# Row values spread by VectorE, and V of four head groups made 512 columns wide in two rounds over its weights

## The chip, the cores and the metric

The kernel runs on one core of one Trainium2 chip. The metric is the device time of one execution in microseconds; several executions are timed and their median counts. One further execution is profiled, and its trace is what the views below are taken from.

## The reference

Two attention layers with 32 heads of 32 columns, on 2048 rows of width 1024 each, and their outputs side by side. Layer A looks at 8 keys, two positions apart; layer B at a sliding block of 256 keys:

```
qkv = (x @ wqkv).reshape(B, S, 3, H, Dh)
# A: keys at s, s-2, ..., s-14
logits = einsum("bhsd,bhswd->bhsw", q, kg) * scale
attn = softmax(where(mask, logits, -1e9));  o = einsum("bhsw,bhswd->bhsd", attn, vg)
# B: 0 <= s - t < 256
scores = einsum("bhqd,bhkd->bhqk", q, k) * scale
p = softmax(where(mask, scores, -1e9));     o = einsum("bhqk,bhkd->bhqd", p, v)
out = concatenate([A: o @ wo, B: o @ wo], axis=-1)
```

All of it is float32.

## The kernel before

**Units and groups.** The work is cut into 8 units of 512 rows: four of layer B ("dense"), then four of layer A, whose even and odd rows are sorted apart, so that its dilated window becomes a plain one of 8 ("window"). Each unit has 8 groups of four heads. For one group the kernel computes q and k (`qk_items`, L333 to L424), stacks them in `qst` and `kst`, makes two passes over the scores (`attention` L656, `window` L546), multiplies by V and hands the result to the output product (`o_items`, L487).

**Precision.** A float32 operand is split on the chip into a high and a low part of TensorE's rounded type (`Stream.parts`, L160: a cast, then two subtractions of 512 columns, on VectorE). A product is three matmuls, `TERMS` (L32): high by high, high by low, low by high. In the scores the parts are stacked instead: rows 0 to 95 of `qst` and `kst` hold high and low parts of 32 columns, three deep, written by DMAs on SP's queue (`place`, L369 to L375).

**Two passes and the row values.** The first pass (`first`, L666) computes a block of scores for 128 rows, VectorE finds each row's masked maximum (L686) and ScalarE the sum of exponentials (L691). `log_sum` (L702) makes one number per row of it, again as high and low part. `rows` (L718) transposes these 16 x 2 columns by a matmul with the identity (L720) into 32 rows of PSUM; VectorE copies them to `rt` (L724), and one DMA on SP's queue (L727) lays them as rows 96 and 97 of `qst`. In `kst` these two rows hold ones (L283). So the second pass (`second`, L559 and L755), which contracts over 98 rows, has the row values already subtracted, transposed, and ScalarE needs only an exponential (L573, L770). Four PSUM banks serve scores of both passes and the transposed row values (ring `rs`); one of them is given back when `rt` is copied.

**V.** `VPARTS` (L25) cuts a unit's V into four parts of two groups, 256 columns each. A part (`v_items`, L436) goes through eight slices of the contraction; in each it computes four blocks of 128 rows, two to a PSUM bank, so that two banks (of three in ring `rg`) are in use. The input block is the stationary operand and the weights, 256 columns, the moving one (L464). Its weights are two items of 128x1024. Each finished bank is copied into `vbuf` (L474).

**Weights.** All weights and inputs are one list of items in the order of use. An item is loaded by a DMA on POOL's queue into one of three raw buffers (L137), split on VectorE (L163, L171) and kept in one of three weight buffers. `split_to` has the next item split while the current one is used.

**The order.** The program is straight-line; its order is worked out when it is built. `plan` (L204 to L215) lists the large products: for each unit and slot s the two output products of the unit before (`O_SLOTS`), q and k of group s, and after that the V part that `V_SLOTS` (L26; for unit 0 `V0_SLOTS`, L28) gives to the slot. The inputs of the next unit are split inside the part of slot 7. Four queues of work stand beside each other: row values, second passes, first passes and large products. A loop (L872) always takes the one whose next piece can start first, by a model of the engines (`Clock`, L35) with a duration for each instruction and a due time for each transfer. Instructions are issued to every engine in the order that this loop gives.

Of the kernel before, what the change touches and what calls it, by code (L numbers as in the profile page):

```python
# [7 lines left out]
F32 = mybir.dt.float32  # L8
# [20 lines left out]
NX, NST, NN = 9,1,3  # L29
TAIL, XAT = 4, 1  # L30
C1, C3, CG, CV = 0.108, 0.2, 0.231, 0.242
TERMS = ((0, 0), (0, 1), (1, 0))  # L32
# [2 lines left out]
class Clock:  # L35
# [7 lines left out]
    MOVE = dict(load=(2.12, 0.14), store=(0.64, 0.4), copy=(1.18, 0.56), rows=(0.37, 0.56),  # L43
                halo_out=(0.4, 0.68), halo_in=(0.55, 0.6), halo_few=(0.28, 0.51))

    def __init__(self):
# [134 lines left out]
def kernel(ctx, tc, xs, wqk, wv, wo, outs, units):  # L181
# [48 lines left out]
    for p in plan:  # L230
        ly = units[p[1]][0]
        if p[0] == "o":
            item(p, "w" if p[1] < U - 1 or p[2] < 3 else "xw", wo[ly, p[2]])
        elif p[0] == "v":
            s0, n = VPARTS[p[2]]
            for g in range(n):
                if n == 2:
                    item(p + (g,), "w", wv[ly, s0 + g])
                else:
                    w4 = wv[ly, s0 + g // 2:s0 + g // 2 + 3:2, :, g % 2 * 512:g % 2 * 512 + 512]  # L240
                    item(p + (g,), "w", w4.rearrange("t p c -> p t c"))
# [19 lines left out]
    def constants():  # L261
        def bands(name, n, keep, fill, *conds):
            m = const.tile([P, n], F32, name=name) if isinstance(name, str) else name
            nc.gpsimd.memset(m, keep)
            for step, base, chan in conds:
                nc.gpsimd.affine_select(m, m, pattern=[[step, n]], compare_op=ALU.is_ge, fill=fill, base=base,
                                        channel_multiplier=chan)
            return m

        ident = cst["ident"] = const.tile([P, P], F32R, name="ident")  # L270
        keep = const.tile([P, P], F32, name="keep_d")
        nc.gpsimd.memset(keep, 0.0)
        nc.gpsimd.affine_select(ident, keep, pattern=[[-1, P]], compare_op=ALU.not_equal, fill=1.0, base=0,
                                channel_multiplier=1)
        cst["mask_d"] = bands("mask_d", 384, 0.0, FAR, (1, -1, -1), (-1, 256, 1))
        cst["mask_w"] = bands("mask_w", 136, 0.0, FAR, (1, -1, -1), (-1, 8, 1))
        cst["keep_f"] = bands("keep_f", P, BIG, 0.0, (-1, -1, 1))
        cst["keep_d"] = bands(keep, P, BIG, 0.0, (1, 0, -1))
        cst["keep_w"] = bands("keep_w", 136, BIG, 0.0, (1, 0, -1), (-1, 7, 1))
        ck.use("pool", 3.0, ck.now)  # L280

        def ones():
            zero = cst["mask_d"][96:98, None, P:2 * P].to_broadcast([2, 24, P])  # L283
            for t in kst:
                nc.scalar.activation(t[96:98, :, :].rearrange("p j (a s) -> p (j a) s", s=P), zero, AF.Identity,
                                     bias=1.0, scale=1.0)
                ck.use("act", 2.7, ck.now)

        ck.defer(13.0, ones)
# [43 lines left out]
    def qk_items(u, s):  # L333
# [12 lines left out]
        def evac(t, ps, bank):  # L346
# [5 lines left out]
            def low():  # L352
# [83 lines left out]
    def v_items(u, part):  # L436


        out = []
        h = {}  # L440
        s0, ng = VPARTS[part]
        nb, per = ng, 4 // ng
        kw = NK // ng

        def ready(k, b):
            if k % kw == 0 and b == 0:
                st.split_to(where["v", u, part, k // kw] + 1)
                h["r"] = st.ready[where["v", u, part, k // kw]]
            if k == NK - 1 and u and any((u - 1) * NG + i not in done["o"] for i in range(s0, s0 + ng)):
                return None  # L450
            return latest(h["r"], rg.when()) if k == 0 else h["r"]

        def run(k, b):
            if k == 0:
                h[b] = rg.take()
            if k % kw == 0 and b == 0:
                w = st.get(where["v", u, part, k // kw])[0]
                h["w"] = w.rearrange("p a (k f) -> p a k f", k=4) if ng == 2 else \
                    w.rearrange("p a (t k f) -> p a k t f", t=2, k=2)
            for r in range(per):  # L460
                for i, (a, c) in enumerate(TERMS):
                    p0 = (per * b + r) * P
                    ps = h[b][0] if per == 1 else h[b][0][:, 256 * r:256 * r + 256]
                    nc.tensor.matmul(ps, xt[u][k][:, a, p0:p0 + P],  # L464
                                     h["w"][:, c, k % kw], start=(k == 0 and i == 0 and r == 0),
                                     stop=(k == NK - 1 and i == 2), skip_group_check=True)
            if k % kw == kw // 2 - (ng == 2) and b == 0 and \
                    st.items[min(where["v", u, part, k // kw] + 1, len(st.items) - 1)][0] != "x":
                st.split_to(where["v", u, part, k // kw] + 2)

        def after(k, b):
            if k == NK - 1:
                c = (4 * u + per * b) % 6
                t = copy_out(vbuf[part][:, c:c + per, :], h[b][0].rearrange("p (a f) -> p a f", a=per), h[b][1], rg)  # L474
                done["vt", b] = t
                if b == nb - 1:
                    done["v"][u, part] = max(done["vt", i] for i in range(nb))

        for k in range(NK):
            for b in range(nb):  # L480
                out.append((lambda k=k, b=b: ready(k, b), lambda k=k, b=b: run(k, b), 3 * (CV if ng == 2 else CG),
                            lambda k=k, b=b: after(k, b)))
        return out

    stores = {}
# [60 lines left out]
    def window(u, s, h):  # L546
# [12 lines left out]
        def second(ki, hp):  # L559
# [3 lines left out]
            ps, bank = rs.take()  # L563
            for i in range(pack):
                j = hp * pack + i
                nc.tensor.matmul(ps[:, i * n:(i + 1) * n], kk[0:98, j, 256 + kb * P:256 + (kb + 1) * P],  # L566
                                 q[0:98, j, q0:q0 + n], start=True, stop=True)
# [49 lines left out]
        def seconds(ki):  # L617
            pack = kbs[ki][3]
            for hp in range(4 // pack):
                two.append(Item(lambda: latest(rs.when(), h["rows"]),  # L620
                                lambda ki=ki, hp=hp: second(ki, hp), pack * C1))

        for ki in range(nk):
# [32 lines left out]
    def attention(u, s):  # L656
# [61 lines left out]
        def rows(hl):  # L718
            ps, bank = rs.take()
            nc.tensor.matmul(ps[0:32, 0:P], hl.rearrange("p a b -> p (a b)"), cst["ident"], start=True, stop=True)  # L720
            rt = small.tile([32, P], F32R, tag="rt", name="rt")

            def copy():
                nc.vector.tensor_copy(rt, ps[0:32, 0:P])  # L724
                e = ck.use("dve", 0.2, ck.now)
                rs.give(bank, e)
                nc.sync.dma_start(q[96:98, :, :].bitcast(F32), rt.bitcast(F32))  # L727
                h["rows"] = ck.copy("rows", e)

            return copy  # L730

        for b in range(4):
            for j in range(4):
# [21 lines left out]
        def second(ki, hp):  # L755
# [4 lines left out]
                h["left", ki, pr] = 2 // pack  # L760
            ps, bank = rs.take()
            for i, j in enumerate(heads):
                nc.tensor.matmul(ps[:, i * n:(i + 1) * n], kk[0:98, j, 256 + kb * P:256 + (kb + 1) * P],  # L763
                                 q[0:98, j, q0:q0 + n], start=True, stop=True)
# [178 lines left out]
```

## Time and profile before

| | us |
|---|---|
| median of three timed runs | 1946.54 |
| lowest and highest | 1946.42, 1950.07 |
| profiled execution | 1951.22 |
| its span, first to last instruction | 1949.5 |
| granted clock of TensorE, mean share | 0.995 |
| DMA queues: SP and ScalarE (hardware), POOL (software) | 26.0 + 3.0% and 23.2% of 16 engines' span |
| first passes: scores' matmuls, L681 | 232.6 busy, 1024 of them |
| second passes: L763 and L566 | 133.4 and 74.7 busy, 704 and 576 |
| masked maxima on VectorE, L686 | 262.4 (dense) and 142.0 (window) busy |
| split of weights on VectorE, L163 and L171 | 173.1 and 328.0 busy |

In the views a line names an engine, the kernel's line, the operation and its tiles (out<-in), the shapes, how many there are, the busy time and the mean duration of one in ns. PE is TensorE's matmuls, PEld its weight loads, DVE VectorE, ACT ScalarE, POOL GpSimd, SP SyncE; a trailing q means the engine's sequencer, which issues DMAs. A mean duration contains the latency of one instruction; where instructions of a kind follow each other, the distance of their starts is shorter.

### The profile page before, as it was taken

The page shows a single profiled execution, that of the slowest core. Times are in us where ns is not written, and L with a number is a line of the kernel's source. Part 1 is how long each engine was busy: PE and PEld are TensorE (multiplying, and loading weights), DVE is VectorE, ACT ScalarE, POOL GpSimd, SP SyncE. Part 2 cuts the span into 40 slices and gives each one's busy share as a digit, 9 for nine tenths or more (in the row PEclk, how much of TensorE's full clock was granted, in tenths as well). Part 3 has the DMA queues.
Part 4 walks back from the last instruction along what each step waited for, and adds up shares of the span by engine and source line. Part 5 has one row for each costly group of instructions (what it writes and reads, how often), then busy time and mean ns, then how long its engine had stood idle before and what let it go on. Part 6 is the DMA issues. An engine that isn't in the chain of part 4 may idle for free. (4 is left out here: it accounts for less than half of the span.)

```text
span 1949.5 us, 35937 instructions
## 1 busy us (share of the span) xinstructions
PE 1904.4 (98%) x12608; PEld 1608.6 (83%) x12608; DVE 1261.6 (65%) x3733; ACT 960.6 (49%) x3136; POOL 375.8 (19%) x958
## 2 busy tenths in 40 slices
PE   8999999999999999999999999999999999999999
PEld 6787787788877888778878888888888788888887
DVE  6667566667666676666755667656676566765673
ACT  3555565655565656565655333433444343434441
POOL 1222222323332323232431001000010000000010
PEclk9999999999999999999999999999999999999999
DMA  6456555455545464555454556545564556546451
GB/s 200 131 141 174 134 147 166 136 150 174 144 141 166 133 185 120 144 147 144 134 147 118 173 164 188 157 133 169 148 182 128 169 158 174 167 130 176 138 157 66
DMA packets 136500, 294.90 MB, mean 151 GB/s; under 512 B 14464, under 2 KB 42112, under 8 KB 136320
## 3 DMA queue, kind: packets, MB, share of 16 engines
q1 hardware_dynamic: 85632, 124.82, 26.0%
q0 software_dynamic: 40320, 146.82, 23.2%
q10 hardware_dynamic: 10368, 20.98, 3.0%
q8 instruction: 100, 1.64, 0.4%
q14 instruction: 80, 0.66, 0.1%
HBM read 163.58 MB, written 27.26 MB: 98 GB/s over the span
## 5 line engine op out<-in xcount | busy, mean ns | idle before, releaser
L412 PE MATMUL g<-x,w 128*128 128x512 f32 x3072 | 799.2, 398 | 9.3 <-DVE w L163 9.0
L412 PEld LDWEIGHTS g<-x,w 128*128 128x128 f32 x3072 | 556.9, 189 | 109.3 <-DVE w L163 10.2
L691 ACT ACTIVATE s<-s,nm 128x384 f32<-128x384 f32 (+3 forms) x1024 | 452.2, 442 | 269.1 <-DVE nm L686 261.0
L464 PE MATMUL g<-w,x 128*128 128x256 f32 x3072 | 411.8, 285 | 0.0
L464 PEld LDWEIGHTS g<-w,x 128*128 128x128 f32 x3072 | 392.9, 192 | 2.0 <-issue 0.2
L686 DVE CUSTOM_DVE_ANT_0 s<-s,mask_d 128x384 f32<-128x384 f32 (+2 forms) x512 | 262.4, 555 | 188.5 <-PE s L681 187.7
L510 PE MATMUL g<-ot,w 128*128 128x512 f32 x1416 | 356.7, 396 | 2.7 <-ACT ot L644 2.3
L171 DVE TENSOR_TENSOR w<-raw,w 128x512 fp32r<-128x512 f32 x502 | 328.0, 695 | 8.7
L510 PEld LDWEIGHTS g<-ot,w 128*128 128x128 f32 x1416 | 258.5, 189 | 53.6 <-ACT ot L644 3.3
L749 POOL TENSOR_SCALAR_AFFINE_SELECT pbuf<-pbuf 128x128 f32<-128x128 f32 (+1 forms) x643 | 219.0, 372 | 296.9 <-ACT pbuf L770 295.8
L681 PE MATMUL s<-kst,qst 96*128 96x384 f32 (+3 forms) x1024 | 232.6, 302 | 15.7 <-DMA kst<-nat 9.7
L770 ACT ACTIVATE pbuf<-s 128x384 f32<-128x384 f32 (+2 forms) x480 | 201.9, 503 | 65.8 <-PE s L763 62.6
L681 PEld LDWEIGHTS s<-kst,qst 96*128 96x128 f32 x1024 | 178.4, 190 | 55.6 <-issue 18.2
L686 DVE CUSTOM_DVE_ANT_0 s<-s,mask_w 128x136 f32<-128x136 f32 (+1 forms) x512 | 142.0, 321 | 113.2 <-PE s L681 112.8
L691 ACT ACTIVATION_READ_ACCUMULATOR s<-s,nm 128x1 f32 x1024 | 209.9, 205 | 0.0
L349 ACT ACTIVATE nat<-g 128x512 fp32r<-128x512 f32 x128 | 76.6, 599 | 249.7 <-PE g L412 245.4
L137 POOL DMA_DIRECT2D raw<-wqk x126 | 68.0, 540 | 572.7 <-DVE w L171 218.2
L353 DVE SCALAR_TENSOR_TENSOR nat<-g,nat 128x512 fp32r<-128x512 f32 x128 | 88.3, 690 | 139.1 <-ACT nat L349 136.2
L163 DVE CAST w<-raw 128x1024 fp32r<-128x1024 f32 x251 | 173.1, 690 | 7.3 <-DMA raw<-wqk 7.3
L686 DVE DVE_READ_ACCUMULATOR2_ANT nm<- 128x1 f32 x1024 | 143.7, 140 | 0.0
L763 PEld LDWEIGHTS s<-qst,kst 98*128 98x128 f32 x704 | 109.0, 189 | 40.4 <-ACT s L691 19.6
L583 DVE TENSOR_TENSOR pbuf<-pbuf,keep_w 128x272 f32<-128x272 f32 (+1 forms) x224 | 95.5, 471 | 70.1 <-ACT pbuf L573 69.8
(53 smaller groups left out, 1071.3 us busy)
## 6 DMA issues: line engine op xcount, KB each, us to landing
raw<-wqk POOLq DMA_DIRECT2D x126, 512.0 KB, 3.7
qst<-nat SPq DMA_DIRECT2D x192, 256.0 KB
kst<-nat SPq DMA_DIRECT2D x192, 256.0 KB
raw<-wo POOLq DMA_DIRECT2D x64, 512.0 KB, 3.7
raw<-wv POOLq DMA_DIRECT2D x62, 512.0 KB, 3.7
raw<-xs POOLq DMA_DIRECT2D x28, 512.0 KB, 4.7
outs<-ost ACTq DMA_DIRECT2D x56, 256.0 KB
halo<-nat SPq DMA_DIRECT2D x40, 256.0 KB
```

The costliest lines, as they stand in the source:

```text
L163: nc.vector.tensor_copy(t[:, 0, :], raw)
L171: nc.vector.tensor_tensor(o, a, b, op=ALU.subtract)
L412: nc.tensor.matmul(h["ps"], h["w"][:, a, k * P:(k + 1) * P], xt[u][k][:, b, :], start=(k == 0 and i == 0), stop=(k == NK - 1 and i == 2))
L464: nc.tensor.matmul(ps, xt[u][k][:, a, p0:p0 + P], h["w"][:, c, k % kw], start=(k == 0 and i == 0 and r == 0), stop=(k == NK - 1 and i == 2 ...
L510: nc.tensor.matmul(h["ps"], w[:, a, c:c + P], ot[u, k][:, b, :], start=(k == 0 and i == 0), stop=(k == NK - 1 and i == 2))
L583: nc.vector.tensor_tensor(w, w, cst["keep_w"][:, None, :n].to_broadcast([P, pack, n]), op=ALU.min)
L681: nc.tensor.matmul(ps[:, :n], q[0:96, j, b * P:(b + 1) * P], kk[0:96, j, c0:c1], start=True, stop=True)
L686: nc.vector.tensor_tensor_reduce(ps[:, :n], ps[:, :n], mask[:, cut:full], scale=-1.0, scalar=BIG, op0=ALU.add, op1=ALU.min, accum_out=nm)
L691: nc.scalar.activation(ps[:, :n], ps[:, :n], AF.Exp, bias=nm, scale=-1.0, accum_out=sm)
L749: nc.gpsimd.affine_select(w, w, pattern=[[0, m], [step, n]], compare_op=ALU.is_ge, fill=0.0, base=base, channel_multiplier=chan)
L763: nc.tensor.matmul(ps[:, i * n:(i + 1) * n], kk[0:98, j, 256 + kb * P:256 + (kb + 1) * P], q[0:98, j, q0:q0 + n], start=True, stop=True)
L770: nc.scalar.activation(w, ps[:, :pack * n].rearrange("p (j n) -> p j n", j=pack), AF.Exp)
```

## The change

Row values: the copy to `rt` and its DMA go away. Rows 96 to 127 of `qst` are now written by VectorE straight from PSUM, for each of the four heads one multiplication of the 32 transposed rows, repeated for the four blocks of 128 rows, by a 0/1 table `pick` that keeps, for head j and block b, rows 4j+b and 16+4j+b. `kst` has ones in all of rows 96 to 127, and the second pass contracts over all 128 rows. A second pass may start when the rows of its last head are there, by the planner's model.

Keys: the planner takes a group's stacked keys to be ready 1.2 us later than before (`KEYS_LATE`).

V: the first four groups of a unit are one part of 512 columns (`VPARTS`), in slot 0; the parts of groups 4, 5 and 6, 7 stay as they were, in slots 5 and 7 (in unit 0 in slots 3 and 7). The wide part runs in two rounds of two row blocks, each block with a PSUM bank of its own. Its weights are four items, each with two slices of the contraction for all 512 columns. Round one goes through items 0, 1, 2, 3; round two uses 1, 2, 3, which are still in the weight buffers, and then item 0, loaded and split a second time as a fifth item. A slice of an item is a moving operand of two pieces of 256 columns, 512 apart. A V piece now also waits, in the model, for the split of the unit's inputs.

```diff
-VPARTS = ((0,2),(2,2),(4,2),(6,2))
-V_SLOTS = {0: 0, 1: 1, 5: 2, 7: 3}
+ROWS_LATE, KEYS_LATE = 0, 1.2
+VPARTS = ((0,4),(4,2),(6,2))
+V_SLOTS = {0:0,5:1,7:2}
-V0_SLOTS = {0:0,2:1,4:2,7:3}
+V0_SLOTS = {0:0,3:1,7:2}
...
-            for g in range(n):
+            for i, g in enumerate((0, 1) if n == 2 else (0, 1, 2, 3, 0)):
...
+        pick = cst["pick"] = const.tile([32, 16], F32, name="pick")
+        nc.gpsimd.memset(pick, 0.0)
+        for row in (0, 16):
+            nc.gpsimd.affine_select(pick, pick, pattern=[[-1, 16]], compare_op=ALU.not_equal, fill=1.0, base=-row,
+                                    channel_multiplier=1)
...
-                        done["stack"][u, s] = max(e2, h2["hi"])
+                        done["stack"][u, s] = max(e2, h2["hi"]) + KEYS_LATE
...
+        wide = ng == 4
+        kw = 2 if wide else 4
+        rounds = [[(0, 0), (1, 1), (2, 2), (3, 3)], [(1, None), (2, None), (3, None), (0, 4)]] if wide else \
+            [[(0, 0), (1, 1)]]
...
+            for half in range(1 if wide else 2):
+                for t, (a, c) in enumerate(TERMS):
+                    p0 = (2 * r + b if wide else 2 * b + half) * P
+                    ps = h[b][0] if wide else h[b][0][:, 256 * half:256 * half + 256]
+                    nc.tensor.matmul(ps, xt[u][kw * g + k][:, a, p0:p0 + P], h["w"][g][:, c, k],
+                                     start=(first and t == 0 and half == 0), stop=(last and t == 2),
+                                     skip_group_check=True)
+            done_block = k == kw - 1 and b == 1
+            if wide and r == 0:
+                if k == 0 and b == 1 and n < 3:
+                    ahead(item_of(n + 1))
+            elif wide:
+                if done_block and n == 0:
+                    ahead(item_of(4))
+                if k == 0 and b == 1 and n == 3:
+                    ahead(item_of(4) + 1)
+            elif k == 1 and b == 0:
+                ahead(item_of(n) + 1)
+
+        def ahead(i):
+            if st.items[min(i, len(st.items) - 1)][0] != "x":
+                st.split_to(i + 1)
...
-                nc.tensor.matmul(ps[:, i * n:(i + 1) * n], kk[0:98, j, 256 + kb * P:256 + (kb + 1) * P],
-                                 q[0:98, j, q0:q0 + n], start=True, stop=True)
+                nc.tensor.matmul(ps[:, i * n:(i + 1) * n], kk[:, j, 256 + kb * P:256 + (kb + 1) * P],
+                                 q[:, j, q0:q0 + n], start=True, stop=True)
...
-            rt = small.tile([32, P], F32R, tag="rt", name="rt")
-
-            def copy():
-                nc.vector.tensor_copy(rt, ps[0:32, 0:P])
-                e = ck.use("dve", 0.2, ck.now)
+            def spread():
+                h["rows"] = []
+                for j in range(4):
+                    nc.vector.tensor_tensor(q[96:P, j, :].rearrange("p (b s) -> p b s", s=P),
+                                            ps[0:32, None, 0:P].to_broadcast([32, 4, P]),
+                                            cst["pick"][0:32, 4 * j:4 * j + 4, None].to_broadcast([32, 4, P]), op=ALU.mult)
+                    e = ck.use("dve", 0.61, ck.now)
+                    h["rows"].append(e + ROWS_LATE)
                 rs.give(bank, e)
-                nc.sync.dma_start(q[96:98, :, :].bitcast(F32), rt.bitcast(F32))
-                h["rows"] = ck.copy("rows", e)
...
-            return latest(rs.when(), h["rows"])
+            return latest(rs.when(), h["rows"] and h["rows"][hp * pack + pack - 1])
```

More of the change, by code (lines that the diff above doesn't have):

```diff
@@ L42 @@
     HOLD = dict(sp=0.63, act=0.35, pool=0.6)
-    MOVE = dict(load=(2.12, 0.14), store=(0.64, 0.4), copy=(1.18, 0.56), rows=(0.37, 0.56),
+    MOVE = dict(load=(2.12, 0.14), store=(0.64, 0.4), copy=(1.18, 0.56),
                 halo_out=(0.4, 0.68), halo_in=(0.55, 0.6), halo_few=(0.28, 0.51))
@@ L282, in ones @@
         def ones():
[L283 removed]
+            zero = cst["mask_d"][96:P, None, P:2 * P].to_broadcast([32, 24, P])
             for t in kst:
[L285 removed]
+                nc.scalar.activation(t[96:P, :, :].rearrange("p j (a s) -> p (j a) s", s=P), zero, AF.Identity,
                                      bias=1.0, scale=1.0)
@@ L439, in v_items @@
         out = []
-        h = {}
+        h = {"w": {}}
         s0, ng = VPARTS[part]
[L442 to L449, printed above, removed]
-                return None
-            return latest(h["r"], rg.when()) if k == 0 else h["r"]
@@ L453, in run @@
-        def run(k, b):
-            if k == 0:
-                h[b] = rg.take()
[L456 to L469, printed above, removed]
@@ L471, in after @@
-        def after(k, b):
-            if k == NK - 1:
-                c = (4 * u + per * b) % 6
-                t = copy_out(vbuf[part][:, c:c + per, :], h[b][0].rearrange("p (a f) -> p a f", a=per), h[b][1], rg)
[L475 to L482, printed above, removed]
+        wide = ng == 4
@@ new lines, in v_items, with item_of, ready @@
+        kw = 2 if wide else 4
+        rounds = [[(0, 0), (1, 1), (2, 2), (3, 3)], [(1, None), (2, None), (3, None), (0, 4)]] if wide else \
+            [[(0, 0), (1, 1)]]
+        def item_of(i):
+            return where["v", u, part, i]
+        def ready(r, n, k, b):
+            g, i = rounds[r][n]
+            if k == 0 and b == 0 and i is not None:
+                st.split_to(item_of(i) + 1)
+                h["r"] = st.ready[item_of(i)]
+            if n == len(rounds[r]) - 1 and k == kw - 1 and u and \
+                    any((u - 1) * NG + i not in done["o"] for i in range(s0, s0 + ng)):
+                return None
+            return latest(h["r"], rg.when(), xready[u][kw * g + k]) if n == 0 and k == 0 else \
+                max(h["r"], xready[u][kw * g + k])
@@ new lines, in run @@
+        def run(r, n, k, b):
+            g, i = rounds[r][n]
+            if n == 0 and k == 0:
+                h[b] = rg.take()
+            if k == 0 and b == 0 and i is not None:
+                w = st.get(item_of(i))[0]
+                h["w"][g] = w.rearrange("p a (t k f) -> p a k t f", t=2, k=2) if wide else \
+                    w.rearrange("p a (k f) -> p a k f", k=kw)
+            first, last = n == 0 and k == 0, n == len(rounds[r]) - 1 and k == kw - 1
+            for half in range(1 if wide else 2):
[16 more added lines that the diff above has]
+                ahead(item_of(n) + 1)
@@ new lines, in ahead, with after @@
+        def ahead(i):
+            if st.items[min(i, len(st.items) - 1)][0] != "x":
+                st.split_to(i + 1)
+        def after(r, n, k, b):
+            if n == len(rounds[r]) - 1 and k == kw - 1:
+                per = 1 if wide else 2
+                c = (4 * u + (2 * r + b if wide else 2 * b)) % 6
+                t = copy_out(vbuf[part][:, c:c + per, :], h[b][0].rearrange("p (a f) -> p a f", a=per), h[b][1], rg)
+                done["vt", r, b] = t
+                if b == 1 and r == len(rounds) - 1:
+                    done["v"][u, part] = max(done["vt", x, y] for x in range(len(rounds)) for y in range(2))
@@ L483, in v_items @@
+        for r in range(len(rounds)):
+            for n in range(len(rounds[r])):
+                for k in range(kw):
+                    for b in range(2):
+                        at = (r, n, k, b)
+                        out.append((lambda at=at: ready(*at), lambda at=at: run(*at), 3 * (CG if wide else CV),
+                                    lambda at=at: after(*at)))
         return out
@@ L619, in seconds @@
             for hp in range(4 // pack):
-                two.append(Item(lambda: latest(rs.when(), h["rows"]),
+                two.append(Item(lambda hp=hp: latest(rs.when(), h["rows"] and h["rows"][hp * pack + pack - 1]),
                                 lambda ki=ki, hp=hp: second(ki, hp), pack * C1))
@@ L720, in rows @@
             nc.tensor.matmul(ps[0:32, 0:P], hl.rearrange("p a b -> p (a b)"), cst["ident"], start=True, stop=True)
-            rt = small.tile([32, P], F32R, tag="rt", name="rt")
-            def copy():
-                nc.vector.tensor_copy(rt, ps[0:32, 0:P])
-                e = ck.use("dve", 0.2, ck.now)
+            def spread():
[6 more added lines that the diff above has]
+                    h["rows"].append(e + ROWS_LATE)
                 rs.give(bank, e)
-                nc.sync.dma_start(q[96:98, :, :].bitcast(F32), rt.bitcast(F32))
-                h["rows"] = ck.copy("rows", e)
-            return copy
+            return spread
         for b in range(4):
@@ L762, in second @@
             for i, j in enumerate(heads):
-                nc.tensor.matmul(ps[:, i * n:(i + 1) * n], kk[0:98, j, 256 + kb * P:256 + (kb + 1) * P],
-                                 q[0:98, j, q0:q0 + n], start=True, stop=True)
+                nc.tensor.matmul(ps[:, i * n:(i + 1) * n], kk[:, j, 256 + kb * P:256 + (kb + 1) * P],
+                                 q[:, j, q0:q0 + n], start=True, stop=True)
             w = pbuf[:, heads[0]:heads[0] + pack, at[ki]:at[ki] + n]
```

6 lines of the change are left out of this document (3 added, 3 removed).

## The prediction

> **What bounds the kernel now.** I read the head of the page first: shares of the engines, the granted clock, and the chain of work that ended last.
>
> ```profile
> span 1949.5 us, 35937 instructions
> PE 1904.4 (98%) x12608; PEld 1608.6 (83%) x12608; DVE 1261.6 (65%) x3733; ACT 960.6 (49%) x3136; POOL 375.8 (19%) x958
> ...
> PEclk9999999999999999999999999999999999999999
> ...
> PE 21%; DMA 1%; DVE 1%; ACT 0%; issue 0%
> PE g L412 8%; PE g L510 6%; PE g L464 4%; PE s L566 1%; PE s L681 1%; PE o L607 1%; DMA qst<-rt 0%; DMA kst<-nat 0%; PE s L510 0%; DVE w L171 0%; DVE w L163 0%; DVE pbuf L583 0%; DVE s L686 0%; ACT s L691 0%; ACT nat L349 0%
> ```
>
> TensorE is busy in 98% of the span at a practically full clock, and nearly all of the traced chain is TensorE's own matmuls. So the time changes in two ways only: TensorE's work gets shorter, or its few waits get longer or shorter. VectorE, at 65%, is next. The waits, from the view of who waited for whom:
>
> ```profile
> PE s L681 <- DMA kst<-nat: 9.7, 6, 2.5
> PE g L412 <- DVE w L163: 9.0, 3, 8.1
> PE s L763 <- DMA qst<-rt: 5.3, 4, 1.8
> PE s L681 <- ACT s L691: 5.2, 5, 1.6
> PE s L566 <- DMA qst<-rt: 3.0, 3, 1.7
> ...
> PEld s L763 <- ACT s L691: 19.6, 29, 2.2
> ...
> PEld s L681 <- ACT s L691: 11.0, 25, 1.8
> ```
>
> The columns are total us, times and the longest. The 8.1 us under L412 is the first weight at the start, which the change doesn't touch. Transfers of row values cost 5.3 + 3.0 = 8.3 us in seven waits, transfers of keys 9.7 us in six. Third, VectorE's spare time is not even. At the seven joints between units it splits the next unit's inputs, and there it is full:
>
> ```profile
> 180.00:190.00 10.00, 7.47 (x63) 7.29 (x62) 9.72 (x27) 2.24 (x10) 2.22 (x4) 1.00 0.91 261
> 440.00:450.00 10.00, 10.00 (x93) 9.56 (x95) 9.83 (x22) 5.19 (x14) 5.58 (x10) 1.00 0.65 197
> 700.00:710.00 10.00, 10.00 (x92) 8.95 (x90) 9.79 (x24) 4.72 (x13) 6.38 (x12) 1.00 0.67 213
> ...
> 1660.00:1670.00 10.00, 9.17 (x56) 7.97 (x54) 9.76 (x30) 3.79 (x16) 1.58 (x3) 1.00 0.57 193
> sum 70.00, PE 65.64 PEld 60.05 DVE 68.15 ACT 27.60 POOL 21.22; mean PE 9.38 PEld 8.58 DVE 9.74 ACT 3.94 POOL 3.03
> ```
>
> After the window come the busy times of PE, PEld, DVE, ACT and POOL. VectorE is busy 9.74 us of each 10 on average, and TensorE already loses 4.4 us in these seven windows.
>
> **Wide V, TensorE's side.** For head groups 0 to 3 of each unit, two matmuls of 256 columns become one of 512. The rate of each comes from the timeline, from a run's start to the next run's start:
>
> ```profile
> L464 PE MATMUL g<-w,x 128*128 128x256 f32 x3072 | 411.8, 285 | 0.0
> ```
>
> ```profile
> 27.79 6.88 PE L464 MATMUL g<-w,x 128*128 128x256 f32 x56
> 34.51 0.86 PE L412 MATMUL g<-x,w 128*128 128x512 f32 x3
> ```
>
> ```profile
> 499.79 4.27 PE L412 MATMUL g<-x,w 128*128 128x512 f32 x18
> 503.90 0.22 PE L720 MATMUL s<-ident,hl 128*32 128x128 f32 x1
> ```
>
> 256 columns: (34.51 - 27.79) / 56 = 120 ns, a pair 240. 512 columns: (503.90 - 499.79) / 18 = 228 ns. Half of the 3072 matmuls are concerned, 768 pairs, so at most 768 x 12 ns = 9.2 us. V is interleaved with scores in runs of six; there the borders of a run count, and they are as many as before. I take 8 us. Bounds: 0 (the wide moving operand is two pieces of 256 columns, 512 apart, a form that the trace doesn't show) and 9.2.
>
> The Trainium skill, "TensorE: Matmul & The Clock Gate", section "Back-to-back issue gap", speaks against it: a warm gap of N/2.4 plus about 2.5 ns has a pair at 218 and one wide matmul at 216 ns, an estimated 2 us for 768 pairs instead of 8. The trace disagrees with it at both widths (120 and 228 ns beside 109 and 216).
>
> **Wide V, the fifth load.** Three weight buffers can't hold four items through both rounds, so item 0 is loaded and split again: 8 units x one item. A split is a cast and two subtractions:
>
> ```profile
> 440.50 1.29 DVE L171 TENSOR_TENSOR w<-raw,w 128x512 fp32r<-128x512 f32 x2
> 441.71 0.69 DVE L163 CAST w<-raw 128x1024 fp32r<-128x1024 f32 x1
> 442.43 1.50 DVE L171 TENSOR_TENSOR w<-raw,w 128x512 fp32r<-128x512 f32 x2
> ```
>
> (442.43 - 441.71) + (441.71 - 440.50) = 0.72 + 1.21 = 1.93 us of VectorE, 15.4 us in eight units, and one more issue on POOL's queue per unit. One wide part lasts 96 x 228 ns = 22 us on TensorE and asks for 5 x 1.93 = 9.7 us of splits, 44% of VectorE, where two narrow parts asked for four in 23 us, 34%. It stands in slot 0, behind the joint. I count it as nothing: it is hidden behind 22 us of matmuls. Without that cover it costs 15.4 us, and the upper bound is that.
>
> **Wide V, the order.** Values of group 0 now wait for a part of 22 us instead of 11.5, since its four groups share one tile; group 1 no longer has a V part behind its keys. Its scores run beside the following output items instead. TensorE has matmuls throughout, so 0, between a loss of the 10 us of the third rival and no gain.
>
> **Row values by VectorE.** Removed per group: one copy and one DMA on SP's queue. Added: four multiplications of 32x512 from PSUM into partitions 96 to 127. What the old way takes:
>
> ```profile
> 82.09 0.27 DVE L724 CAST rt<-s 32x128 fp32r<-32x128 f32 x1
> ...
> 82.39 0.68 SPq L727 DMA_DIRECT2D qst<-rt  x1
> ...
> 86.75 0.42 PE L763 MATMUL s<-qst,kst 98*128 98x384 f32 x1 [1.80 <-DMA qst<-rt]
> ```
>
> From the copy's start to the first second-pass matmul 4.66 us, of which TensorE waits 1.80. VectorE's time goes by columns, not partitions, as these rows show:
>
> ```profile
> L431 DVE COPY vbuf<-g 128x512 f32<-128x512 f32 x16 | 11.1, 691 | 23.8 <-PE g L464 23.8
> L724 DVE CAST rt<-s 32x128 fp32r<-32x128 f32 x64 | 17.7, 277 | 39.3 <-PE s L720 39.3
> ```
>
> 32x128 takes 277 ns, 128x512 from PSUM 691. In a row such operations follow each other every 605 ns (half of 1.21 above). So the spread takes 4 x 0.605 = 2.4 us, of which the first two heads are ready after 1.3. Both are less than 4.66 by over 2 us, more than the longest of the seven waits (1.8): the 8.3 us go. I take 8; bounds 0 (the spread queues behind a split in a full VectorE, 1.93 us) and 8.3. The contraction over 128 instead of 98 rows costs TensorE nothing: a load of 128 columns takes 189 to 190 ns at 96, 98 and 128 rows.
>
> ```profile
> L681 PEld LDWEIGHTS s<-kst,qst 96*128 96x128 f32 x1024 | 178.4, 190 | 55.6 <-issue 18.2 <-ACT s L691 11.0 <-ACT pbuf L770 0.6
> L763 PEld LDWEIGHTS s<-qst,kst 98*128 98x128 f32 x704 | 109.0, 189 | 40.4 <-ACT s L691 19.6 <-issue 8.9 <-PE o L810 0.8
> L412 PEld LDWEIGHTS g<-x,w 128*128 128x128 f32 x3072 | 556.9, 189 | 109.3 <-DVE w L163 10.2 <-issue 2.4 <-DVE w L171 1.7
> ```
>
> VectorE pays 64 x (2.4 - 0.2) = 141 us more. With the 15.4 it goes to 1418 us, 73% of the span: hidden on the whole, behind TensorE. Not hidden at the joints. A spread comes once per about 30 us (1949.5 / 64) and the full stretch lasts some 15 us, so about half of the seven are hit: 3.5 x 2.2 = 8 us, as each delay there lengthens a wait that TensorE already has. Queued behind a spread are the maximum of the next scores (L686), so their PSUM bank, and the next split, so POOL's next load. The bank of the row values itself is held 2.4 instead of some 0.3 us, one of four: I add 2 us for it, between 0 and 10 (a third more of the 19.6 + 11.0 us that weight loads for scores wait for ACT to free a bank).
>
> **Later keys.** The planner now believes keys 1.2 us later and puts other matmuls ahead. Six waits of 9.7 us, the longest 2.5: I take half, 4 us off; bounds 9.7 off and, if a first pass is simply put later with nothing else to run, 0.
>
> **Sum.** The profiled execution took 1951.22 us (span 1949.5 and 1.7 around it). 1951.2 - 8 (V) - 8 (rows) - 4 (keys) + 8 (joints) + 2 (bank) = 1941.2. That execution stands 0.24% above the median of the three timed runs, 1946.54; scaled by 1946.54 / 1951.22 the sum is **1936.6**.
>
> **The rivals.**
>
> *VectorE becomes the bound at the joints.* For it: 9.74 of 10 us there, and TensorE's 4.4 us. Every joint then pays the spread's 2.2 us and the fifth item's 1.93, since that item follows in the next slot: 7 x 4.1 = 29 us, with V and rows gained and the keys late as before: 1951.2 - 16 + 29 = 1964, scaled 1960. It decides if VectorE's full stretch lasts from the joint into the wide part, over some 30 us. Against it: V's items come 4.5 us apart.
>
> *The wide matmul is no faster than two narrow ones.* Then V gives 0: 1949.2, scaled 1944.5. For it the two-piece operand, against it L412's 228 ns with a plain one. By the Trainium skill's formula quoted above the part is 2 us, and the whole 1942.6.
>
> *The gain is given back by banks and order.* Score banks held longer and group 0's values late cost 10 us instead of 2: 1949.2, scaled 1944.5; with the keys' waits unchanged 1948.5. Against it: output and V matmuls are there to fill.
>
> *More is gained.* All DMA waits go and nothing is lost at the joints: 1951.2 - 9.2 - 8.3 - 9.7 = 1924, scaled 1919.5. The relief of SP's queue, 64 issues fewer, speaks for it.
>
> **How the numbers follow.** Forecast 0.44, its own range 1927 to 1942; joints 0.24; no faster matmul 0.12; given back 0.10; more gained 0.10. About 0.2%, 4 us, is what can be told from no change. Faster: 0.44 + 0.10 and a third of the no-faster-matmul case, 0.58. Same: the other two thirds and the given-back case, 0.18. Slower: 0.24. The range of 8 in 10 goes from 1922, which leaves out half of the case of more gained, to 1958, which leaves out over half of the joints'.
>
> **What would show it.** V's 512-wide runs at 228 ns start to start, and 1536 matmuls fewer of 256 columns. No wait for a transfer of row values, and a second pass starting some 1.3 to 2.5 us after the first spread. VectorE near 1418 us. TensorE's time in the seven joints: if it falls clearly below 65 of 70 us, the joints' rival is at work. Wrong would be a wide matmul at 240 ns, a spread over 0.7 us each, or new waits of TensorE on VectorE's splits.

## The result, and the profile after

| | before | after |
|---|---|---|
| median, us (4 runs each) | 1947.35 | 1927.51 |
| lowest and highest | 1946.42, 1950.07 | 1926.3, 1929.16 |
| ratio, 95% interval | | 0.9896, 0.9879 to 0.9914 |
| profiled execution, span | 1951.22, 1949.5 | 1927.66, 1926.0 |

The changed kernel is 1.0% faster, 20 us. That is within the range, below the forecast (1936.6) and at the lower edge of the forecast's own range (1927 to 1942). In one run below, the one with the order kept, one of four executions took 2636.68 us at a granted clock of 0.654 and is left out of its figures. The head of the page of the changed kernel, which answers to the rows of engines shown above:

```profile
span 1926.0 us, 34516 instructions
...
PE 1897.7 (99%) x11840; PEld 1565.1 (81%) x11840; DVE 1430.3 (74%) x3989; ACT 965.1 (50%) x3139; POOL 385.7 (20%) x926
```

TensorE issues 768 matmuls fewer, but its busy time falls by only 6.7 us of the 23.5 us of span. The rest is idle time: 45.1 us of span without a matmul before (1949.5 - 1904.4), 28.3 after. The view of who waited for whom says which waits are left:

```profile
PE g L418 <- DVE w L164: 8.2, 2, 7.9
PE s L714 <- ACT s L724: 4.4, 5, 1.6
PE s L753 <- DVE hl L745: 3.2, 5, 1.6
PE s L799 <- ACT s L724: 2.6, 5, 0.6
PE s L753 <- ACT s L724: 1.9, 2, 1.0
PE s L799 <- ACT pbuf L806: 1.0, 2, 0.6
PE s L714 <- DMA kst<-nat: 0.7, 1, 0.7
...
PE s L799 <- DVE qst L759: 0.2, 1, 0.2
```

Row values: 8.3 us of waits on transfers before, 0.2 us on the spread after. Keys: 9.7 before, 0.7 after. The 8 us at the start stay. How one spread lies beside TensorE's work, from the timeline of the changed kernel:

```profile
88.74 0.22 PE L753 MATMUL s<-ident,hl 128*32 128x128 f32 x1
...
88.97 0.86 PE L418 MATMUL g<-x,w 128*128 128x512 f32 x3
89.04 2.48 DVE L759 TENSOR_TENSOR qst<-s,pick 32x512 fp32r<-32x512 f32 x4
...
90.59 2.31 PE L481 MATMUL g<-w,x 128*128 128x256 f32 x18
92.75 0.34 PE L799 MATMUL s<-qst,kst 128*128 128x384 f32 x1
```

Four multiplications in 2.48 us; TensorE is in V's matmuls when they end and comes to the second pass 1.2 us later without a wait.

For a finer account than the busy shares, all distances from one matmul's start to the next matmul's start were added up by stage; gaps in which TensorE had no matmul are taken out as idle, and matmuls started at half clock as a stage of their own (us):

```
kernel            idle  half clock    qk      V   first  second  values      o
before            41.4     15.9     728.2  371.7  145.2   161.2   120.7  356.8
after             24.6      9.6     728.5  369.3  145.9   163.8   120.8  355.3
rows_keys         24.2      9.6     728.6  372.4  145.6   160.1   121.1  356.0
order_narrow      25.9      6.8     728.6  372.7  146.7   163.8   121.9  356.8
wide_alone        50.6     20.2     725.2  368.0  144.9   162.7   122.1  356.2
spread_twice_told 85.3    111.9     717.2  358.0  146.3   161.1   119.2  354.8
```

From before to after: idle -16.8, time at half clock -6.3, V -2.4, second passes +2.6, the rest within 1.5 each. The V columns do not hold all of V, though: before, 27 of its 3072 matmuls ran at half clock and stand in that column, after none of the 2304. At the 122 ns that the others took, these 27 need 3.3 us at full clock. Counted so, V is 375.0 us before, its gain is 5.7 us, and what the half clock itself gives back is some 3 us. So V, which gives the change its name, is a quarter of the gain, and the second passes take nearly half of it back.

### The profile page after: what moved, and what is told of

It reads as the page before. It is cut to its first block, busy times and chain, and to the rows that moved or that the text cites. A ratio compares the mean times of both kernels' runs of the same rounds, so it can differ in the third digit from the quotient of the medians.

```text
span 1926.0 us, 34516 instructions
## 1 busy us (share of the span) xinstructions
PE 1897.7 (99%) x11840; PEld 1565.1 (81%) x11840; DVE 1430.3 (74%) x3989; ACT 965.1 (50%) x3139; POOL 385.7 (20%) x926
## 5 line engine op out<-in xcount | busy, mean ns | idle before, releaser
L481 PE MATMUL g<-w,x 128*128 128x256 f32 (+1 forms) x2304 | 404.6, 322 | 0.9 <-DVE w L172 0.7
L481 PEld LDWEIGHTS g<-w,x 128*128 128x128 f32 x2304 | 332.5, 190 | 26.6 <-DVE w L172 2.5
L172 DVE TENSOR_TENSOR w<-raw,w 128x512 fp32r<-128x512 f32 x518 | 339.7, 697 | 8.9
L785 POOL TENSOR_SCALAR_AFFINE_SELECT pbuf<-pbuf 128x128 f32<-128x128 f32 (+1 forms) x600 | 213.8, 384 | 313.0 <-ACT pbuf L806 303.0
L714 PE MATMUL s<-kst,qst 96*128 96x384 f32 (+3 forms) x1024 | 238.0, 302 | 5.6 <-ACT s L724 4.4
L714 PEld LDWEIGHTS s<-kst,qst 96*128 96x128 f32 x1024 | 182.5, 189 | 51.8 <-ACT s L724 10.8
L759 DVE TENSOR_TENSOR qst<-s,pick 32x512 fp32r<-32x512 f32 x256 | 158.4, 675 | 37.9 <-PE s L753 37.0
L164 DVE CAST w<-raw 128x1024 fp32r<-128x1024 f32 x259 | 179.3, 692 | 7.0 <-DMA raw<-wv 4.0
L799 PEld LDWEIGHTS s<-qst,kst 128*128 128x128 f32 x704 | 112.8, 189 | 42.6 <-ACT s L724 14.9
```

Source lines behind the costliest of these rows:

```text
L164: nc.vector.tensor_copy(t[:, 0, :], raw)
L172: nc.vector.tensor_tensor(o, a, b, op=ALU.subtract)
L481: nc.tensor.matmul(ps, xt[u][kw * g + k][:, a, p0:p0 + P], h["w"][g][:, c, k], start=(first and t == 0 and half == 0), stop=(last and t == 2),
L714: nc.tensor.matmul(ps[:, :n], q[0:96, j, b * P:(b + 1) * P], kk[0:96, j, c0:c1], start=True, stop=True)
L759: nc.vector.tensor_tensor(q[96:P, j, :].rearrange("p (b s) -> p b s", s=P), ps[0:32, None, 0:P].to_broadcast([32, 4, P]), cst["pick"][0:32 ...
L785: nc.gpsimd.affine_select(w, w, pattern=[[0, m], [step, n]], compare_op=ALU.is_ge, fill=0.0, base=base, channel_multiplier=chan)
```

## The experiments

The theory: three gains on TensorE's path, each by itself: 7 us of V's work, 8 us of waits for row transfers, 9 us for keys. The rivals: that the planner's new order is the cause, that the parts interact, or that VectorE pays at the joints. Six runs build the three parts alone and in pairs, so that with the kernels before and after there are all eight combinations. Ratios are to the kernel before on the same chip.

**Row values alone.** The changed kernel with these lines as before:

```diff
-ROWS_LATE, KEYS_LATE = 0, 1.2
-VPARTS = ((0,4),(4,2),(6,2))
-V_SLOTS = {0:0,5:1,7:2}
-V0_SLOTS = {0:0,3:1,7:2}
+ROWS_LATE, KEYS_LATE = 0, 0
+VPARTS = ((0,2),(2,2),(4,2),(6,2))
+V_SLOTS = {0: 0, 1: 1, 5: 2, 7: 3}
+V0_SLOTS = {0:0,2:1,4:2,7:3}
```

This kernel also keeps the change's rule that a V piece waits, in the model, for the split of the unit's inputs.

> Only the row values by VectorE; V in four narrow parts and the keys' due time as before. Theory A (three separate gains: 7 us of TensorE's work from the wide V, 8 us of waits for row transfers, 9 us of waits for keys): about 8 us less than before, 1939 us; no wait of a second pass on a transfer; VectorE about 1415 us busy; the waits for keys (9.7 us before) stay within a few us. Rival B (the new order made by the planner takes the waits away, not the shorter path of the row values): no clear gain, 1944 to 1950. Rival C (the spread costs at the joints): 1950 or more.

1941.93 us, ratio 0.9955 (0.9939 to 0.9971). The transfers' waits are gone, but the spread has waits of its own:

```profile
PE s L599 <- DVE qst L759: 4.9, 3, 1.6
PE s L799 <- DVE qst L759: 4.7, 1, 4.7
...
PE s L714 <- DMA kst<-nat: 3.0, 2, 1.6
```

So the size fits theory A while the mechanism fits it in part only: 9.6 us of waits on the spread stand in place of 8.3 on transfers, and the keys' waits fell by 6.7 us in the new order. Rival B is not excluded by this run.

**The same with the order kept.** The planner is told the copy's 0.2 us and the old transfer, so that, constants apart, every engine but VectorE and SP gets its instructions as before:

```diff
-                    e = ck.use("dve", 0.61, ck.now)
-                    h["rows"].append(e + ROWS_LATE)
-                rs.give(bank, e)
+                e = ck.use("dve", 0.2, ck.now)
+                rs.give(bank, e)
+                h["rows"] = [ck.copy("rows", e)] * 4
```

> Row values by VectorE, but the planner is told the old duration and due time (copy of 0.2 us and the DMA), so that TensorE runs its instructions in exactly the order of before. Theory A: the seven waits of 8.3 us for row transfers go, with the order unchanged; VectorE's 140 us more are not seen, 1938 to 1941. Rival B (it was the order): 1946 or more, because the spread, 2.4 us instead of 0.3, delays maxima and splits that the order does not provide for.

1975.59 us, ratio 1.0125 (1.0108 to 1.0142), far on the rival's side. The view of waits:

```profile
PE s L714 <- DVE qst L759: 20.5, 20, 1.9
```

Not one second pass waits for row values, as theory A says. But the first pass (L714) does, twenty times: it is next in the order, needs a score bank, and the bank of the row values is free only after the spread's 2.5 us: in the trace each of the twenty starts 0.15 us after the last multiplication ends. So the bank, which I had put at 2 us, costs 20 us where the order doesn't provide for it. The shorter path pays only in an order that is planned for it; the two are one gain, not two.

**Keys alone.** The kernel before with `max(e2, h2["hi"]) + 1.2` as due time of the keys.

> Only the keys' due time moved by 1.2 us in the planner's model; nothing else is changed in what is computed or moved. Theory A: the waits for keys fall from 9.7 to some 2 us and the time by 6 to 9 us, 1938 to 1941. Rival (a first pass is only put later and TensorE has nothing else to run): waits on others take their place, 1945 to 1949.

1941.84 us, ratio 0.9954 (0.9938 to 0.9971). Keys' waits 1.1 us instead of 9.7:

```profile
PE s L721 <- DVE hl L713: 3.8, 5, 1.0
PE s L764 <- DMA qst<-rt: 3.5, 4, 1.7
PE s L567 <- DMA qst<-rt: 3.5, 5, 1.2
...
PE s L682 <- DMA kst<-nat: 1.1, 2, 0.9
```

A fall of 9 us, the upper end of what theory A says; the row transfers' waits stay (7.0). A change of one number in the planner is worth as much as the spread.

**Wide V alone.** The kernel before with the new `VPARTS`, slots and `v_items`.

> Only the wide V with its fifth load; row values by copy and DMA, keys' due time as before. Theory A: TensorE's matmuls of V take about 7 us less (from 412 to 405 busy), the two kinds of DMA waits stay near 18 us together: 1940 us. Rival (the order with the wide part is what removes the waits): 1925 to 1932, with waits for transfers below 8 us. Rival (the fifth split of 1.9 us a unit is felt): 1947 or more.

1960.68 us, ratio 1.0048 (1.0033 to 1.0063): slower. Theory A falls here. V's start-to-start time drops as it should (368.0 instead of 371.7 in the account above, with 13 and 27 of its matmuls in the half-clock column), and idle time grows by 9.2 us:

```profile
PE s L709 <- DMA kst<-nat: 9.3, 6, 2.5
...
PE s L791 <- DMA qst<-rt: 6.4, 4, 2.2
PE s L594 <- DMA qst<-rt: 6.1, 9, 1.7
...
PE s L709 <- DMA qst<-rt: 2.8, 1, 2.8
PE s L709 <- DMA kst<-halo: 2.2, 1, 2.2
```

In the order with the wide part TensorE comes to transfers of row values too early more often: 15.3 us in 14 waits, 8.3 in seven before. So the gain isn't missing. My reading is that it is spent on waits that the planner doesn't see; the pairs below test that.

**The pairs.** After that run the theory was: the wide part saves its matmuls but exposes every transfer that the planner takes for earlier than it is; rows and keys take one kind each away.

> The changed kernel with the keys' due time as before: row values by VectorE and the wide V. Theory A (the wide V saves its 7 us always, but each transfer that the planner takes for earlier than it is costs more waits beside it; rows and keys each take one kind of these waits away): no waits for row transfers, some 9 us for keys as in the wide V alone, ratio to before 0.992 to 0.998. Rival (the parts add up as measured alone, 0.9955 x 1.0048): 1.000 or above.

> Wide V and the keys' later due time; row values by copy and DMA as before. Theory A: the waits for keys go (9.3 us in the wide V alone), those for row transfers stay at 8 to 15 us, ratio to before 0.993 to 0.998. Rival (the parts add up, 1.0048 x 0.9954): 1.000 or above.

> Row values by VectorE and the keys' later due time, V in four narrow parts. Theory A: both kinds of waits are gone already, so that only the 7 us of V are missing to the changed kernel: ratio to before 0.992 to 0.995, TensorE idle about 30 us, busy about 1903. Rival (the wide order itself is needed, since it moves V to where TensorE waits): ratio 0.996 to 1.000.

Without the later keys: 1948.64 us, 0.9988 (0.9978 to 0.9997). With the rows by DMA: 1948.17, 0.9992 (0.9978 to 1.0006). Both lie between the two expectations. Rows and keys without wide V: 1931.03, 0.9899 (0.9884 to 0.9914), below theory A's 0.992. Its head, and its longest waits of TensorE's matmuls:

```profile
span 1926.5 us, 36059 instructions
...
PE 1898.2 (99%) x12608; PEld 1607.5 (83%) x12608; DVE 1412.4 (73%) x3956; ACT 961.2 (50%) x3135; POOL 377.9 (20%) x931
```

```profile
PE g L418 <- DVE w L164: 8.0, 1, 8.0
PE s L753 <- DVE hl L745: 4.4, 4, 3.5
PE s L714 <- ACT s L724: 3.9, 4, 1.6
```

No wait of a matmul on a transfer or on the spread is in its list. The whole gain is there without the wide V. In a table of ratios:

| | V narrow | V wide |
|---|---|---|
| neither | 1 | 1.0048 |
| rows | 0.9955 | 0.9988 |
| keys | 0.9954 | 0.9992 |
| rows and keys | 0.9899 | 0.9896 |

Down a column, rows and keys add up in narrow V (0.9955 x 0.9954 = 0.9909) and gain more than that in wide V (the product with 1.0048 would be 0.9932, measured 0.9896). Across, the wide part costs 0.3 to 0.5% in three rows and nothing in the fourth. With the keys but not the rows, the waits on row transfers are 17.4 us (10.1 and 7.3), which fits the theory. With rows but not keys it fits less: one wait of 2.6 us for keys, and 7.9 us in five waits of the transposition on VectorE, with 32.7 us at half clock beside 21.2 in rows alone. What sets those waits wasn't tried.

**Is the width itself worth anything?** Three kernels more on one chip: the changed kernel, the one with rows and keys, and the changed kernel in exactly its order, with each wide matmul issued as two of 256 columns:

```diff
-            for half in range(1 if wide else 2):
+            for half in range(2):
...
-                    ps = h[b][0] if wide else h[b][0][:, 256 * half:256 * half + 256]
-                    nc.tensor.matmul(ps, xt[u][kw * g + k][:, a, p0:p0 + P], h["w"][g][:, c, k],
+                    ps = h[b][0][:, 256 * half:256 * half + 256]
+                    nc.tensor.matmul(ps, xt[u][kw * g + k][:, a, p0:p0 + P],
+                                     h["w"][g][:, c, k, half] if wide else h["w"][g][:, c, k],
```

> The changed kernel once more, beside the next three on one chip. Ratio to before 0.988 to 0.991. If the wide V is worth its 3 us of matmuls (369 instead of 372 us of start-to-start time), it is 0.1 to 0.2% below the kernel with rows and keys alone; if its gain is given back by its order, the two are equal within 0.1%.

> Rows by VectorE and later keys, V in narrow parts, on the same chip as the changed kernel. Wide V worth 3 us: 0.1 to 0.2% slower than the changed kernel, ratio to before 0.990 to 0.992. Given back: equal to it.

> The changed kernel with exactly its order of instructions on every engine, but each 512-column matmul of V issued as two of 256, as before. If the wide matmul saves what the start-to-start times say (7 ns a pair on 768 pairs at most), this is 3 to 5 us slower than the changed kernel; by the prediction's 12 ns a pair, 9 us slower; by a formula of N/2.4 plus 2.5 ns, 2 us. If it is only 1 us or less slower, the width is hidden.

| | median, us | ratio, 95% interval |
|---|---|---|
| changed kernel | 1927.71 | 0.9879, 0.9862 to 0.9896 |
| rows and keys, narrow V | 1930.17 | 0.9891, 0.9875 to 0.9907 |
| changed kernel's order, narrow matmuls | 1933.36 | 0.9914, 0.9899 to 0.9929 |

With the order equal, the width is worth 5.7 us of the medians, the intervals just apart. That is between the expectation's 3 to 5 us and its 9. V's start-to-start times in the two profiles of this call are 372.7 us (narrow) and 369.5 (wide), but 15 of the 3072 narrow matmuls ran at half clock and stand in that column. With all 3072 at the mean of the others V would be 374.5 us, so that 5.0 of the 5.7 us are found.

The order with its fifth load costs 3.2 us against narrow parts, by the medians; these two intervals overlap. In the account above the difference stands in the second passes: 163.8 us in both kernels of the wide order, 160.1 with narrow parts. Why they take longer wasn't tried, nor the fifth load apart from the order. What is left, 2.5 us between the changed kernel and the one without wide V, is inside the intervals.

One stretch says little about the width. The first V part, from the timelines of the changed kernel (its first profile) and of the narrow matmuls in its order:

```profile
22.78 10.15 PE L481 MATMUL g<-w,x 128*128 128x512 f32 x42
```

```profile
23.28 10.23 PE L481 MATMUL g<-w,x 128*128 128x256 f32 x84
```

The last matmul's own length (some 0.40 and 0.28 us) left out, 9.75 / 41 = 238 ns for a wide one and 9.95 / 83 = 120 ns for a narrow one: in this stretch a pair gains 2 ns. Over all V matmuls at full clock with no idle gap behind them the mean is 237 ns for a wide one and 122 for a narrow one (medians 231 and 120), and a pair gains some 6 ns: not 2, and not 12.

**How much more can VectorE take?** Each multiplication done twice, first with the planner told 0.61 us for each, then 0.70, near what the repeated ones took (they start 0.71 us after the first):

```diff
+                    for _ in range(2):
                         nc.vector.tensor_tensor(q[96:P, j, :].rearrange("p (b s) -> p b s", s=P),
...
-                    e = ck.use("dve", 0.61, ck.now)
+                        e = ck.use("dve", 0.70, ck.now)
```

> The changed kernel with each of the four multiplications done twice, which the planner counts: VectorE gets some 155 us more, 1585 of 1930 us, 82%. Theory A (VectorE has room, also at the joints between units): within 6 us of the changed kernel, ratio to before 0.988 to 0.993. Rival (the joints pay for what VectorE gets, 2.4 us for each spread that falls there): 8 to 17 us slower than the changed kernel, ratio 0.994 to 0.998, with TensorE's waits in the joints grown.

> Each multiplication of the spread twice, as in the run where this cost 5%, but the planner is told 0.70 us for each (what the second onto the same rows took) instead of 0.61. If that loss came from the planner's order running ahead of VectorE, most of it goes: below 1.02 of before, waits of second passes on the spread below 10 us. If VectorE itself has no room for it, 1.03 to 1.05 stay, with TensorE idle over 60 us.

2045.37 us, 1.0511 (1.0452 to 1.0571), and 2062.91, 1.0566 (1.0547 to 1.0586). Both theories of the first expectation are far off, and of the second the one in which VectorE has no room is the nearer, though the loss is above its 1.05 too. The second kernel's head and waits:

```profile
PE 1972.4 (96%) x11840; PEld 1606.2 (78%) x11840; DVE 1601.4 (78%) x4232; ACT 968.1 (47%) x3140; POOL 399.0 (19%) x938
```

```profile
PE s L800 <- DVE qst L760: 24.9, 12, 3.9
PE s L599 <- DVE qst L760: 14.0, 7, 4.4
PE s L753 <- DVE hl L745: 10.8, 5, 2.6
PE s L800 <- ACT pbuf L807: 10.0, 16, 0.8
```

VectorE is at 78%, and TensorE waits on its spread. By the account above, the span's 136 us over the changed kernel are 61 us more of idle time and 102 us more at half clock, less 27 us of work that moved from the other columns to the half clock. Little of it lies at the joints: in seven stretches of 25 us there TensorE loses 19.4 us, 7.6 in the changed kernel. So VectorE's average says little. My reading is that it counts how long the spread stands between the first and the second pass of a group. In the changed kernel it takes 2.5 us, where the copy, the transfer and the start of the second pass took 4.7 in the prediction's stretch; done twice it takes 5.35. That this length, and not VectorE's other work behind it, makes the loss is argued and not separated.

## Why the prediction was right, and where its terms were off

The mechanism held: TensorE is the bound, it lost its waits for transfers, and VectorE's 169 us more were not seen. The size held less well: the result lies at the edge of the forecast's own range, because most of the errors below lean the same way. The sum's terms, each against what was measured (profiled executions; predicted -10.0, measured -23.6):

- *V, -8.* Mis-sized: some -5, from -5.0 with the order fixed to -5.7 from before to after, and 5.7 us of the medians with the order fixed. The step that failed is the rate: 228 ns, read from one run of 18 matmuls, was taken for that of a 512-column matmul. Their mean is 237 ns beside 122 for a narrow one, so the prediction's own sign of being wrong, 240 ns, was nearly met, and a pair gains some 6 ns instead of 12. The Trainium skill, "TensorE: Matmul & The Clock Gate", section "Back-to-back issue gap", by which the estimate was 2 us, was as far off on the other side; its absolute gaps (109 and 216 ns) agree with neither width.
- *The fifth load, 0, and the order, 0.* Together some 3 us of loss (order with narrow matmuls against narrow parts), inside the bounds given; in the account it is the second passes. That the order could cost 0.5% when rows and keys are absent was not foreseen in any part.
- *Row values, -8.* Right in size for the whole change, 8.3 to 0.2 us of waits, and 4 x 0.605 was 2.48 us. The mean of one multiplication, 675 ns for 32x512, is close to the 691 of 128x512, so that the prediction's reading by columns held. The step from a shorter path to 8 us less was too short, though: the same path lost in the old order, and by itself it gained its 9 us with 9.6 us of waits on the spread, while the keys' waits fell. In the stretch shown the second pass came 3.7 us after the spread's start, not the 1.3 to 2.5 that the prediction names, since TensorE had other matmuls in between. VectorE's busy time came to 1430, 12 above the 1418.
- *Keys, -4.* Mis-sized: -9.0. Taking half of the waits was a guess between two bounds, and the upper bound was the answer.
- *Joints, +8.* Wrong. The step was that a full VectorE at the joints makes TensorE wait longer. In the 25 us from the first split of the next unit's inputs, before and after:

```profile
444.00:469.00 25.00, 23.93 (x179) 19.38 (x178) 21.27 (x57) 12.38 (x35) 8.37 (x18) 1.00 0.77 217
...
sum 175.00, PE 162.06 PEld 137.21 DVE 140.06 ACT 83.56 POOL 43.81; mean PE 23.15 PEld 19.60 DVE 20.01 ACT 11.94 POOL 6.26
```

```profile
442.00:467.00 25.00, 23.71 (x168) 19.04 (x167) 23.02 (x58) 11.95 (x34) 9.30 (x19) 1.00 0.70 210
...
sum 175.00, PE 167.37 PEld 139.95 DVE 161.54 ACT 82.10 POOL 49.53; mean PE 23.91 PEld 19.99 DVE 23.08 ACT 11.73 POOL 7.08
```

VectorE goes from 20.0 to 23.1 us of 25, and TensorE loses 7.6 us in the seven joints instead of 12.9. Among the 12.9 were waits for transfers, which went, and waits for splits did not come in their place: in the whole execution V's matmuls wait 0.7 us for a subtraction (L172), and those of q and k 8.2 us for a weight's cast, nearly all of it for the first weight. That these transfers make the whole difference wasn't tried.

- *Score bank, +2.* Not there: weight loads for scores waited 25.7 us for ACT instead of 30.6. Its price without the planner's knowledge is the 20 us above.
- *Not in the sum: the clock.* Time at half clock fell by 6.3 us, which is worth about 3 us.

With -5.7, -8, -9, -3 for the clock and +2.6 for the second passes the sum is -23, and the rest is below a microsecond. The rival "more gained" described the waits better than the forecast did. The likeliest sign, faster, was right mostly through the waits for two kinds of transfer; the width saved about 5 us, and its order gave 3 of them back.

## What to carry to other kernels

In a kernel whose bound engine is 98% busy, look first at the few waits left, and ask which of them exist because a planner's due time is too early: here one constant was worth as much as a rewritten stage. Test the parts of a compound change alone and in pairs; here the wide V was a loss by itself and about nothing beside the others, because its order cost most of what its width saved. A rate for a price should come from all instructions of a form, not from one run of them. And times summed by stage can be compared only if each stage holds the same instructions in both kernels.

## What the runs showed of the hardware

The clock can halve after quite a short idle stretch. In the changed kernel a first pass waited 1.59 us for a score bank near the end of the last unit:

```profile
1871.37 0.83 PE L714 MATMUL s<-kst,qst 96*128 96x136 f32 x2 [1.59 <-ACT s L724]
```

The windows of 3.4 us there:

```profile
1864.80:1868.20 3.40, 3.40 (x25) 3.10 (x25) 3.33 (x6) 2.56 (x10) 1.29 (x2) 1.00 0.11 18
1868.20:1871.60 3.40, 1.81 (x13) 1.41 (x11) 3.40 (x14) 1.35 (x6) 0.53 (x1) 1.00 0.81 271
1871.60:1875.00 3.40, 3.04 (x43) 2.07 (x42) 1.30 (x10) 1.11 (x5) 0.00 (x0) 0.51 0.06 22
1875.00:1878.40 3.40, 3.07 (x8) 2.53 (x9) 1.88 (x10) 2.29 (x13) 0.00 (x0) 0.50 0.00 0
1878.40:1881.80 3.40, 3.40 (x9) 2.63 (x9) 0.00 (x0) 0.00 (x0) 0.00 (x0) 0.50 0.00 0
1881.80:1885.20 3.40, 3.40 (x17) 2.74 (x16) 2.71 (x5) 0.00 (x0) 0.00 (x0) 0.99 0.00 0
```

A window in which TensorE was busy 1.81 of 3.4 us is followed by three at half clock. TensorE works 9.5 us in these three, and about half of it, some 5 us, is lost by this estimate. In the same kernel run again the place looks alike. But not every such wait is followed by it. Before the change this wait of 2.53 us lies in a stretch, 180 to 190 us, whose granted clock is 1.00 in the prediction's view of the joints:

```profile
184.88 0.63 PE L681 MATMUL s<-kst,qst 96*128 96x128 f32 x4 [2.53 <-DMA kst<-nat]
```

What decides between the two wasn't worked out. The Trainium skill, "TensorE: Matmul & The Clock Gate", section "Why this matters for your kernels", asks for no gaps over some 3 us; here half of that stood ahead of half clock.

In the run with each multiplication done twice, the second one onto the same 32 rows started 0.71 us after the first, where multiplications for different heads follow each other every 0.60 to 0.61 us.
